# Two places in a hand-ordered schedule: the first shared-out unit behind a block, and the sink scores of the slots that end in a block

## The chip, the cores and the metric

The kernel runs on one core of one Trainium2 chip. The metric is the device time of one launch in microseconds, the median of 3 runs: 180.98 us (180.37, 180.98 and 181.20). The engines have short names in the profile: PE is TensorE (matrix products and transposes), PEld its weight loads, DVE is VectorE, ACT is ScalarE, POOL is GpSimd, and SP is the engine that starts most of the transfers. Each engine works through its own list of instructions in the order in which the kernel writes them, and waits on semaphores for the others.

## What is computed

Two layers, one after the other, for 4 sequences of 768 rows. The first is attention with 8 heads of 64 columns, in which a query sees the keys of the last 128 positions and the first 4 positions ("sinks"). The second is a gated block: a matrix product to 1024 columns, a gelu, one half normalised and mixed over the rows with a 768 x 768 matrix, a product of the halves, and a projection back, added to the input.

```
scores = scale * q @ k.T          # 4 x 8 heads, 768 x 768, 64 columns
keep   = (pos_k < 4) | (0 <= pos_q - pos_k < 128)
a      = softmax(where(keep, scores, -1e9));  x = a @ v       # -> 4 x 768 x 512
h      = gelu(x @ w_in);  u, v = halves of h
v_n    = (v - mean) / sqrt(var + 1e-6) * g_ln
v_s    = w_sg @ v_n + b_sg        # over the 768 rows
out    = x + (u * v_s) @ w_out
```

## The kernel before, in words

**Slots.** The main loop (L571) has 16 slots, one for each pair of heads; `n` is the slot, and four slots (HP = 4) make a sequence. A slot writes out, in this order, the work of several stages at once, because every engine keeps to the written order:

- For `g` = 0, 1, 2 (HT = 3): `score(n, g)` (L249) makes the scores of two key tiles on PE into a PSUM tile `sc`, and ACT takes their exponential into `ex` (L264). `keep_band(n, g)` (L266) multiplies that part of `ex` by a mask of ones and zeros on DVE (L271). This is "the mask" in what follows; the mask of `g` waits for the exponential of `g`.
- Between these stand the weighted sums of the pair before (`values`, L288: PE into `av`, then on DVE a reciprocal and the product `x`, L315 and L316), and the keys and queries of the next pair (`keys` L208, `queries` L216: six transposes on PE into `cps`, then a copy on ACT, L204). In a late slot (below) `queries` stands at `g` = 1.
- `sinks(n)` (L273) makes the scores of the sink keys with one 512-column product on PE (`scs`, L275), and ACT takes their exponential (`exs`, L277). It stands behind the three rounds.

The score tiles `sc` and `scs` share two PSUM buffers in turn, so the product that fills one waits for the exponential of the tile two places before.

**Blocks.** In slots 4, 8 and 12 (`n % HP == 0`, `n > 0`) the four pairs of a sequence are complete. There `columns(n - 1)` (L283: six transposes, a copy `xT` on DVE, L286) stands behind the last scores, and at the slot's end comes the block `hidden` (L422): 6 products `hv` (L333) with gelu (L335) and statistics (L337), with 3 of the weighted sums of slot `n` between them; 8 products `hu` (L345) with gelu (L348); and the normalisation `vn` (L373). A gelu needs another table on ACT than an exponential or a copy, and each change is an ACT_TABLE_LOAD.

**Units.** The rest of the second layer is put on a list of units, which later slots share out. Behind the first block these are 6 `spatial_weights` (L177: six transposes of `w_sg` on PE into `wps`, a copy `wsgT` on DVE, L182), behind every block 8 `spatial` (L377: six products `vs` on PE, then `gv`, L386, and `gT`, L389, on DVE) and 6 `project` (L391: four products `o_ps`, a sum `o_sb` on DVE, L401, and a store by SP). `wps`, `vs`, `o_ps`, `hv`, `hu` and, in some places, `cps` share two PSUM buffers of the pool `ps_m` in turn. `spread(left)` (L584) takes the next share off the list: two units at each of the four places of slot 5, one at each place of slot 9.

**Late slots.** The slot behind a block (5, 9 and 13; `late`) has only the second three weighted sums left. It writes, for `g` = 0: scores, keys, the three sums, mask 0, then the first share of units, `spread(HT + 1)`; for `g` = 1: scores, mask 1, the second share, queries; for `g` = 2: scores, mask 2, the third share; then the sinks, and the fourth share. PE has no part in a mask, and the units' products need no mask of their own slot; what a place of the mask decides is DVE's order.

Of the kernel before, what the change touches and what calls it, by code (L numbers as in the profile page):

```python
# [17 lines left out]
def kernel(  # L18
# [14 lines left out]
    nc = tc.nc  # L33

    B, H, S, Dh = q.shape
# [6 lines left out]
    HP = H // 2  # L42
# [18 lines left out]
    HT = NT // 2  # L61
    NS = S - 256
    NB = 2
# [3 lines left out]
    sk_bufs = [consts.tile([128, 128], BF16, name=f"sk{i}") for i in range(NB)]  # L67
# [17 lines left out]
    def load_v(n):  # L85
        b, hp = divmod(n, HP)
        nc.gpsimd.dma_start(  # L87
            out=v_bufs[n % NV][:, :, :, 0:64],
            in_=v[b, 2 * hp:2 * hp + 2].rearrange("h (t p) d -> p h t d", p=128))
# [69 lines left out]
    def load_weights(n):  # L159
        if n < 4:  # L160
            half = slice(DF, d_ff) if n < 2 else slice(0, DF)
            cs = slice(KD // 2 * (n % 2), KD // 2 * (n % 2 + 1))
            nc.gpsimd.dma_start(
                out=w_in_sb[:, cs, half],
                in_=moe_w_in.rearrange("(c p) f -> p c f", p=128)[:, cs, half])
        elif n == 4:
            for c in (slice(0, HT), slice(HT, NT)):
                nc.gpsimd.dma_start(
                    out=wsg_sb[:, c, :],
                    in_=moe_w_sg.rearrange("(c p) s -> p c s", p=128)[:, c, :])  # L170
        elif n == 5:
            nc.gpsimd.dma_start(out=b_bc, in_=moe_b_sg.partition_broadcast(128))
            nc.gpsimd.dma_start(out=g_sb, in_=moe_g_ln.rearrange("(c p) -> p c", p=128))
            nc.gpsimd.dma_start(out=w_out_sb,
                                in_=moe_w_out.rearrange("(c p) f -> p c f", p=128))
# [8 lines left out]
    packed, qTs, exps, avs = {}, {}, {}, {}  # L184
    x_sb, xT = {}, {}

    def repack(n, eng):
        packed[n] = []
        for src, name in zip(qk.pop(n), ("k_bf", "q_bf")):
            flat = work.tile([128, NT, 128], BF16, name=name)  # L190
            eng.tensor_copy(flat.rearrange("p t (h d) -> p h t d", h=2), src)  # L191
            packed[n].append(flat)
# [15 lines left out]
    def keys(n):  # L208
        kT, sk = kT_bufs[n % NB], sk_bufs[n % NB]
        kps = to_columns(packed[n][0], ps_t, "tp")  # L210
        copy(nc.scalar, kT, kps)
        for hl in range(2):
            rows = slice(64 * hl, 64 * hl + 64)
            nc.gpsimd.tensor_copy(sk[rows, 32 * hl:32 * hl + n_sink], kT[rows, 0:n_sink])  # L214

    def queries(n, eng, pool, tag):  # L216
        qps = to_columns(packed.pop(n)[1], pool, tag)
        qTs[n] = work.tile([128, S], BF16, name="qT")
        copy(eng, qTs[n], qps)
# [29 lines left out]
    def score(n, g):  # L249
        kT, qT = kT_bufs[n % NB], qTs[n]  # L250
        if g == 0:
            exps[n] = work.tile([128, NT * 512 - 256], BF16, name="ex")
        ex = exps[n]
        sc = ps_s.tile([128, 2, 512], F32, name="sc", tag="s")
        w = 0
        for j in (2 * g, 2 * g + 1):
            n_q = min(256, S - 128 * j)
            for hl in range(2):
                rows = slice(64 * hl, 64 * hl + 64)
                nc.tensor.matmul(sc[:, hl, w:w + n_q], kT[rows, 128 * j:128 * (j + 1)],  # L260
                                 qT[rows, 128 * j:128 * j + n_q], start=True, stop=True)
            w += n_q
        part = ex[:, 1024 * g:1024 * g + 2 * w].rearrange("p (h c) -> p h c", h=2)
        nc.scalar.activation(out=part, in_=sc[:, :, 0:w], func=AF.Exp, scale=scale)  # L264
# [7 lines left out]

    def sinks(n):  # L273
        scs = ps_s.tile([128, 2, 512], F32, name="scs", tag="s")
        nc.tensor.matmul(scs[:, 0, 0:NS], sk_bufs[n % NB], qTs.pop(n)[:, 256:S],  # L275
                         start=True, stop=True)
        nc.scalar.activation(out=exs_bufs[n % NB][0:32 + n_sink],  # L277
                             in_=scs[0:32 + n_sink, 0, 0:NS], func=AF.Exp, scale=scale)
# [4 lines left out]
    def columns(n, pool=ps_m, tag="mm"):  # L283
        b, hp = divmod(n, HP)
        xps = to_columns(x_sb[b][:, hp], pool, tag)
        nc.vector.tensor_copy(xT[b][:, hp, :], xps.rearrange("c t p -> c (t p)"))  # L286

    def values(n, i):  # L288
        b, hp = divmod(n, HP)
        if hp == 0 and i == 0:  # L290
            x_sb[b] = work.tile([128, HP, NT, 128], BF16, name="x")
            xT[b] = work.tile([128, HP, S], BF16, name="xT")
        ex, exs, v_sb = exps[n], exs_bufs[n % NB], v_bufs[n % NV]
        c, m = divmod(i, HT)
        if m == 0:
            avs[n] = ps_a.tile([128, HT, 2, 65], F32, name="av", tag="av")
        av = avs[n]

        def probs(j, hl, half):
            at = 1024 * (j // 2) + hl * min(512, S - 256 * (j // 2) + 128)  # L300
            at += 256 * (j % 2) + 128 * half
            return ex[:, at:at + 128]

        for hl in range(2):
            nc.tensor.matmul(av[:, m, hl, :], probs(i, hl, 0), v_sb[:, hl, i, :],  # L305
                             start=(m == 0 and hl == 0), stop=False)
            if i >= 1:
                nc.tensor.matmul(av[:, m, hl, :], probs(i - 1, hl, 1),  # L308
                                 v_sb[:, hl, i - 1, :], start=False, stop=False)
        if i >= 2:  # L310
            nc.tensor.matmul(av[:, m], exs[:, 128 * (i - 2):128 * (i - 1)],
                             vsink[:, n], start=False, stop=(m == HT - 1))
        if m == HT - 1:
            rcp = inverses[:, 2 * n + c]
            nc.vector.reciprocal(rcp, av[:, :, :, 64:65])  # L315
            nc.vector.tensor_mul(  # L316
                x_sb[b][:, hp, HT * c:HT * (c + 1), :].rearrange(
                    "p i (h d) -> p i h d", h=2),
                av[:, :, :, 0:64], rcp.to_broadcast([128, HT, 2, 64]))
        if i == NT - 1 and by_dma(n):  # L320
            nc.sync.dma_start_transpose(
                out=xT[b][:, hp, :].rearrange("p (i q) -> p i q", i=NT),
                in_=x_sb[b][:, hp].rearrange("p i d -> p (i d)"))
# [93 lines left out]
    def fill(count=1):  # L417
        for _ in range(count):
            if fillers:
                fillers.pop(0)()  # L420
# [150 lines left out]
    for n in range(NP):  # L571
        if n + 2 < NP:
            repack(n + 2, G)
            load_v(n + 2)
        load_weights(n)
        late = half_valued == n - 1

        def value(i):
            if n > 0 and (i >= HT or not late):
                values(n - 1, i)  # L580

        points = (HT + 1) * ((HP - n) % HP)

        def spread(left):  # L584
            if n > HP * (B - 1):
                fill(1 if left > 2 or (left == 1 and n < NP - 1) else 0)
            else:
                fill(-(-len(fillers) // (points + left)))

        for g in range(HT):  # L590
            if n + g > 0:
                score(n, g)
            if g < 2 and not late:
                for i in range(HT * g, HT * (g + 1)):
                    value(i)
            if g == 0 and n > 0 and n + 1 < NP:
                keys(n + 1)
                if n < HP:
                    queries(n + 1, A, ps_m, "mm")
            if g == 0 and late:  # L600
                for i in range(HT, NT):
                    value(i)
            if g == HT - 1 and n % HP == 0 and n > 0:
                columns(n - 1)
            keep_band(n, g)
            if g == 1 and late:
                spread(HT)
            if g == 1 and n + 1 < NP and n >= HP:
                queries(n + 1, A, ps_t, "tp")
            if g != 1 or not late:  # L610
                spread(HT + 1 - g)
        if n + 3 < NP:
            load_qk(n + 3)
        sinks(n)
        if n == 0:
            keys(1)
            queries(1, A, ps_m, "mm")
        if 0 < n < HP:
            columns(n - 1)
        spread(1)  # L620
        if n % HP == 0 and n > 0:
            fill(len(fillers))
            hidden(n // HP - 1, [lambda i=i: values(n, i) for i in range(HT)])
            half_valued = n
# [58 lines left out]
```

## Time and profile before

| | us |
|---|---|
| median of 3 runs (lowest, highest) | 180.98 (180.37, 181.20) |
| the profiled execution: its time | 180.05 |
| its span, first to last instruction | 178.3 |
| PE busy | 158.1 (89%) |
| DVE busy | 144.2 (81%) |
| ACT busy | 118.9 (67%) |
| POOL busy | 58.2 (33%) |

The span is what the views of the profile cover; 1.75 us of the profiled time lie outside it. All times below that name a place ("at 47.79") are us from the start of the span. In a line of the timeline the first two numbers are start and length, then come engine, line, operation, the tiles written and read, and the number of instructions; a bracket gives the idle time of the engine just before, and what ended it. Slot 5 begins at 43.6, slot 9 at 86.2, slot 13 at 123.5; the blocks before them begin at 31.3, 74.9 and 111.6 with their first `hv`.

### The profile page before, as it was taken

Reading aid. Unit: us, or ns where it says so; the run is one execution under the profiler, and the core shown is the slowest. Engines: PE = TensorE matmul, PEld = TensorE weight load, DVE = VectorE, ACT = ScalarE, POOL = GpSimd, SP = SyncE. Lnnn points to the kernel's source line nnn. Section 1 sums busy time; section 2 is a strip of 40 time slices with the busy share of each in tenths; the row PEclk is TensorE's granted clock in tenths of the full one; section 3 lists DMA queues with packets and bytes.
Section 4 is the critical chain, followed back from the end, with each engine's and each line's share of the span. In section 5 each row is a group of like instructions: output and inputs, shape, how many; then the busy total and the mean of one; then the engine's idle time right before and its main releaser. Section 6 shows DMA issues by size and latency. Waiting matters only on the chain.

```text
span 178.3 us, 3744 instructions
## 1 busy us (share of the span) xinstructions
PE 158.1 (89%) x1407; PEld 89.5 (50%) x1418; DVE 144.2 (81%) x359; ACT 118.9 (67%) x168; POOL 58.2 (33%) x98
## 2 busy tenths in 40 slices
PE   0769779899589999999999999899999999999970
PEld 0447556345456555445556546446465454546430
DVE  5664889599859999878899999599999949858950
ACT  2488999877746677677878678867996756640000
POOL 8549999950042060344007060353020000000000
PEclk9999999999969999999999999999999999999996
DMA  5999999999747539999073969997202241011071
GB/s 155 274 288 272 273 273 272 190 208 220 119 167 48 112 120 185 303 305 76 9 214 30 194 198 179 353 163 45 44 4 46 48 178 59 0 73 50 0 298 62
DMA packets 47974, 27.24 MB, mean 153 GB/s; under 512 B 33680, under 2 KB 44944, under 8 KB 47952
## 3 DMA queue, kind: packets, MB, share of 16 engines
q0 software_dynamic: 27904, 6.31, 37.7%
q1 hardware_dynamic: 19504, 20.26, 37.1%
q10 hardware_dynamic: 544, 0.39, 0.7%
q8 instruction: 12, 0.20, 0.4%
q14 instruction: 10, 0.08, 0.1%
HBM read 24.81 MB, written 6.29 MB: 174 GB/s over the span
## 4 chain that ended last, share of the span: by engine, by line
PE 53%; DVE 25%; ACT 12%; issue 4%; DMA 2%; DVEq 0%
PE hu L345 9%; PE o_ps L397 9%; PE vs L383 8%; PE hv L333 8%; ACT ex L264 6%; DVE gv L386 6%; PE sc L260 5%; DVE ex L271 5%; PE cps L197 4%; DVE gT L389 3%; PE av L305 3%; DVE x L316 3%; ACT qT L204 2%; DVE st L337 2%; DMA k_sb<-in_k_dram 2%
## 5 line engine op out<-in xcount | busy, mean ns | idle before, releaser
L264 ACT ACTIVATE ex<-sc 128x1024 bf16<-128x1024 f32 (+1 forms) x48 | 45.7, 960 | 16.8 <-PE sc L260 16.7
L383 PE MATMUL vs<-wsgT,vn 128*128 128x384 bf16 x192 | 35.8, 329 | 0.7 <-DVE wsgT L182 0.5
L191 POOL CAST k_bf<-k_sb 128x768 bf16<-128x768 f32 x15 | 12.8, 853 | 41.8 <-DMA k_sb<-in_k_dram 24.9
L397 PE MATMUL o_ps<-w_out_sb,gT 128*128 128x512 bf16 (+1 forms) x93 | 23.8, 370 | 0.8 <-DVE o_sb L401 0.4
L383 PEld LDWEIGHTS <-vn 128*128 128x128 bf16 x192 | 17.9, 99 | 13.0 <-issue 2.8
L271 DVE TENSOR_TENSOR ex<-ex,mask 128x1024 bf16<-128x1024 bf16 x32 | 22.6, 708 | 2.2 <-ACT ex L264 2.2
L345 PE MATMUL hu<-xT,w_in_sb 128*128 128x384 bf16 x128 | 23.2, 324 | 0.1
L333 PE MATMUL hv<-w_in_sb,xT 128*128 128x512 bf16 x92 | 22.0, 379 | 1.2 <-ACT v_all L335 0.9
L386 DVE SCALAR_TENSOR_TENSOR gv<-vs,g_sb,b_bc 128x384 bf16<-128x384 f32 x32 | 19.6, 612 | 2.1 <-PE vs L383 2.1
L260 PE MATMUL sc<-qT,kT 64*128 64x256 bf16 x192 | 19.0, 280 | 2.3 <-DVE qT L240 1.3
L337 DVE BATCH_NORM_STATS2 st<-v_all 128x6 f32<-128x512 f32 x24 | 16.2, 676 | 5.6 <-ACT v_all L335 5.6
L348 ACT ACTIVATE uT<-hu 128x384 bf16<-128x384 f32 x32 | 15.7, 491 | 6.5 <-PE hu L345 6.3
L316 DVE TENSOR_TENSOR x<-av,inverses 128x384 bf16<-128x384 f32 x32 | 17.8, 558 | 1.1
L305 PE MATMUL av<-v_sb,ex 128*128 128x65 bf16 x192 | 18.2, 198 | 0.5 <-DVE x L316 0.2
L305 PEld LDWEIGHTS <-ex 128*128 128x128 bf16 x192 | 14.4, 100 | 7.9 <-issue 2.9
L335 ACT ACTIVATE v_all<-hv 128x512 f32<-128x512 f32 x24 | 14.1, 597 | 6.0 <-PE hv L333 6.0
L345 PEld LDWEIGHTS <-w_in_sb 128*128 128x128 bf16 x128 | 12.4, 96 | 10.7 <-issue 2.9
L87 POOL DMA_DIRECT2D v_sb<-in_v_dram x16 | 16.6, 1038 | 0.0
L308 PE MATMUL av<-v_sb,ex 128*128 128x65 bf16 x160 | 16.5, 197 | 0.0
L214 POOL COPY sk<-kT 64x4 bf16<-64x4 bf16 x30 | 6.6, 221 | 29.3 <-ACT kT L204 28.4
L333 PEld LDWEIGHTS <-xT 128*128 128x128 bf16 x96 | 9.1, 98 | 11.3 <-issue 1.4
L191 POOL CAST q_bf<-q_sb 128x768 bf16<-128x768 f32 x15 | 13.9, 930 | 1.7 <-DMA q_sb<-in_q_dram 1.1
(83 smaller groups left out, 241.9 us busy)
## 6 DMA issues: line engine op xcount, KB each, us to landing
k_sb<-in_k_dram SPq DMA_DIRECT2D x15, 384.0 KB, 5.5
q_sb<-in_q_dram SPq DMA_DIRECT2D x15, 384.0 KB, 6.0
out_dram<-o_sb SPq DMA_DIRECT2D x17, 256.0 KB, 3.8
v_sb<-in_v_dram POOLq DMA_DIRECT2D x16, 192.0 KB, 6.6
out_dram<-o_act SPq DMA_DIRECT2D x6, 256.0 KB, 2.0
wsg_sb<-in_moe_w_sg_dram POOLq DMA_DIRECT2D x2, 576.0 KB, 9.8
w_in_sb<-in_moe_w_in_dram POOLq DMA_DIRECT2D x4, 256.0 KB, 8.8
w_out_sb<-in_moe_w_out_dram POOLq DMA_DIRECT2D x1, 512.0 KB, 10.8
```

Of the source, the lines that this page charges most:

```text
L191: eng.tensor_copy(flat.rearrange("p t (h d) -> p h t d", h=2), src)
L260: nc.tensor.matmul(sc[:, hl, w:w + n_q], kT[rows, 128 * j:128 * (j + 1)], qT[rows, 128 * j:128 * j + n_q], start=True, stop=True)
L264: nc.scalar.activation(out=part, in_=sc[:, :, 0:w], func=AF.Exp, scale=scale)
L271: nc.vector.tensor_mul(part, part, m)
L305: nc.tensor.matmul(av[:, m, hl, :], probs(i, hl, 0), v_sb[:, hl, i, :], start=(m == 0 and hl == 0), stop=False)
L316: nc.vector.tensor_mul(x_sb[b][:, hp, HT * c:HT * (c + 1), :].rearrange("p i (h d) -> p i h d", h=2), av[:, :, :, 0:64], rcp.to_broadcast( ...
L333: nc.tensor.matmul(h_ps, xT[b][:, c, 128 * j:128 * (j + 1)], w_in_sb[:, c, DF:], start=(c == 0), stop=(c == KD - 1))
L337: nc.vector.bn_stats(out=st, in_=v_alls[b][:, j, :])
L345: nc.tensor.matmul(h_ps[:, 0:NH], w_in_sb[:, c, 128 * f:128 * (f + 1)], xT[b][:, c, NH * n:NH * (n + 1)], start=(c == 0), stop=(c == KD - 1))
L383: nc.tensor.matmul(vs[:, 0:NH], vns[b][:, si, 128 * f:128 * (f + 1)], wsgT[:, si, cols], start=(si == 0), stop=(si == NT - 1))
L386: nc.vector.scalar_tensor_tensor(out=gv, in0=vs[:, 0:NH], scalar=g_sb[:, f:f + 1], in1=b_bc[:, cols], op0=ALU.mult, op1=ALU.add)
L397: nc.tensor.matmul(o_ps, gTs[b][:, c, rows], w_out_sb[:, c, cols], start=(c == 0), stop=(c == KU - 1 and whole))
```

## The change

In late slots the first share of units is written ahead of mask 0 instead of behind it. In slots 4, 8 and 12 the sinks are written ahead of the third scores instead of behind the third round; in these slots the product `scs` thereby takes the PSUM buffer that the third `sc` had, and the other way round. All other slots keep their order. The number of instructions is the same, and so is the number of units in each share. `sinks` no longer takes `qT` off its table, since the scores behind it still read it; that is bookkeeping of the program that writes the kernel, and no instruction.

```diff
     def sinks(n):
         scs = ps_s.tile([128, 2, 512], F32, name="scs", tag="s")
-        nc.tensor.matmul(scs[:, 0, 0:NS], sk_bufs[n % NB], qTs.pop(n)[:, 256:S],
+        nc.tensor.matmul(scs[:, 0, 0:NS], sk_bufs[n % NB], qTs[n][:, 256:S],
                          start=True, stop=True)
...
         for g in range(HT):
+            if g == HT - 1 and n % HP == 0 and n > 0:
+                sinks(n)
             if n + g > 0:
                 score(n, g)
...
             if g == 0 and late:
                 for i in range(HT, NT):
                     value(i)
+                spread(HT + 1)
             if g == HT - 1 and n % HP == 0 and n > 0:
                 columns(n - 1)
             keep_band(n, g)
...
-            if g != 1 or not late:
+            if g == 2 or not late:
                 spread(HT + 1 - g)
         if n + 3 < NP:
             load_qk(n + 3)
-        sinks(n)
+        if n % HP > 0 or n == 0:
+            sinks(n)
```

## The prediction

> **What bounds the kernel now.** I read the page's busy shares, then the chain of waits, then the timeline around the three blocks, then a table of granted clock by stages. The chain is, by engine:
>
> ```profile
> PE 53%; DVE 25%; ACT 12%; issue 4%; DMA 2%; DVEq 0%
> ```
>
> PE is the floor nearly everywhere; DVE carries the chain from 113 to 141 us. So an edit pays where PE stands still, or where DVE does between 113 and 141. The longest halt that the chain crosses is in slot 5, behind the first block, and the change touches it. The timeline there, with some rows left out:
>
> ```profile
> 45.39 0.56 DVE L316 TENSOR_TENSOR x<-av,inverses 128x384 bf16<-128x384 f32 x1
> ...
> 46.57 0.69 DVE L271 TENSOR_TENSOR ex<-ex,mask 128x1024 bf16<-128x1024 bf16 x1 [0.62 <-ACT ex L264]
> ...
> 47.12 1.04 ACT L264 ACTIVATE ex<-sc 128x1024 bf16<-128x1024 f32 x1
> 47.18 1.02 DVE L182 COPY wsgT<-wps 128x768 bf16<-128x768 bf16 x2
> ...
> 47.79 0.96 PE L180 MATMUL wps<-iden,wsg_sb 128*128 128x128 bf16 x12 [1.81 <-DVE wsgT L182]
> ...
> 48.19 0.69 DVE L271 TENSOR_TENSOR ex<-ex,mask 128x1024 bf16<-128x1024 bf16 x1
> ...
> 48.80 1.01 DVE L182 COPY wsgT<-wps 128x768 bf16<-128x768 bf16 x2
> 49.12 0.80 ACT L204 COPY qT<-cps 128x768 bf16<-128x768 bf16 x1 [0.96 <-PE cps L197]
> 49.81 0.82 ACT L264 ACTIVATE ex<-sc 128x768 bf16<-128x768 f32 x1
> 50.66 0.56 DVE L271 TENSOR_TENSOR ex<-ex,mask_end 128x768 bf16<-128x768 bf16 x1 [0.85 <-ACT ex L264]
> 51.14 1.01 DVE L182 COPY wsgT<-wps 128x768 bf16<-128x768 bf16 x2
> ```
>
> DVE has `x` done at 45.95 and then idles 0.62 us for the exponential behind the table load, although the copies of two finished `wps` stand next. PE, whose third `wps` needs the buffer that the first copy empties, idles 1.81 us. The queries' transposes stand behind that `wps`, so ACT idles 0.96 us ahead of `qT`; so exponential 2 is late, so mask 2 is late (0.85), so the copies behind it, and the first `vs` waits for the fifth of them (51.69) and starts at 51.74.
>
> **Part one, slot 5.** No instruction comes or goes; two copies of 0.55 us (0.47 from start to start) pass mask 0 (0.69). Step by step:
>
> 1. Copies 1 and 2 start at 45.87 and 46.34, 0.48 behind the start of `x`, a spacing that slot 8 has (71.12, 71.60). They end at 46.42 and 46.89. Mask 0 follows at 46.8; its input is there since 46.54, and it is read only in slot 6.
> 2. PE's third and fourth `wps` start at 46.49 and 46.96 instead of 47.79 and 48.25; the transposes of the queries follow at 47.3 instead of 48.58 (their buffer is free when the copy `kT` ends at 47.23).
> 3. ACT is in exponential 1 until 48.16, as before. Then `qT` at 48.05 instead of 49.12, exponential 2 from 48.73 to 49.55 instead of 49.81 to 50.63.
> 4. Mask 1 does not move: it waits for exponential 1 (48.19). Copies 3 and 4 stay at 48.80 and 49.27.
> 5. Mask 2 follows copy 4 directly, at 49.74 instead of 50.66; copies 5 and 6 at 50.22 and 50.69; the first `vs` at 50.83 instead of 51.74. Gain **0.91 us**. Late next is DVE, which is full from mask 1 on.
>
> Behind that, PE was busy 14.73 of the 15 us from 60 to 75, so the gain should be carried on. The transfers do not take it back: `k_sb` for slot 8 is cast at 51.18 and its transposes come in slot 7; the cast at 104.13 is done 1.9 us before its transposes at 107.22, twice the gain. Nothing on SP is passed: the transposing transfer waits for `x`, which stays.
>
> **The clock in this place** is the uncertain term. Windows on the grid of the granted clock:
>
> ```profile
> 25.32:28.73 3.41, 2.36 (x39) 1.61 (x37) 2.85 (x8) 3.37 (x5) 3.29 (x6) 1.00 1.60 254
> ...
> 45.80:49.21 3.41, 1.60 (x26) 1.24 (x22) 2.79 (x6) 2.45 (x4) 0.37 (x2) 1.00 0.65 96
> 49.21:52.62 3.41, 2.90 (x20) 1.89 (x17) 2.10 (x5) 2.01 (x3) 1.31 (x2) 0.50 0.59 213
> ```
>
> The columns are window, length, then busy us of PE, PEld, DVE, ACT, POOL, then the granted clock. A stretch with PE busy 1.60 of 3.41 us was followed by 3.41 us at half clock; one with 2.36 was not. With the steps above the same stretch has some 1.77 (estimate), between the two rows but nearer to the first. If the half-clock stretch stays at its place, transposes go at 0.107 us instead of 0.055 and `scs` at 0.43, so PE itself reaches `vs` only at 51.12; the stretch then covers 1.5 us of `vs` instead of 0.9, and the twelve products end at 53.88 instead of 54.20: gain 0.32. If it goes, the twelve take 2.00 us (0.162 apart) instead of 2.46: gain 0.91 + 0.46 = 1.37. I take 0.91, which leaves the clock's toll as it was, and keep 0.32 and 1.37 as ends.
>
> The Trainium skill, "TensorE: Matmul & The Clock Gate" (Part 1 and Part 4), says that the activity window of about 3.4 us runs freely and that transposes do not count as busy in the same way. By it the stretch would stay slow, since transposes are all that the change draws into it. The 3.41 agrees; whether transposes count no row decides alone (the 1.60 holds 0.37 of other products, the 2.36 holds 1.77).
>
> **Part one, slots 9 and 13.** Slot 9:
>
> ```profile
> 89.16 0.69 DVE L271 TENSOR_TENSOR ex<-ex,mask 128x1024 bf16<-128x1024 bf16 x1 [0.77 <-ACT ex L264]
> ...
> 89.70 1.04 ACT L264 ACTIVATE ex<-sc 128x1024 bf16<-128x1024 f32 x1
> ...
> 90.77 0.69 DVE L271 TENSOR_TENSOR ex<-ex,mask 128x1024 bf16<-128x1024 bf16 x1
> ```
>
> `gv` and `gT` can use the 0.77 us: `vs` is done at 88.54. But mask 1 waits for exponential 1, which ends at 90.74; it stays at 90.77, and so does all behind it. PE is in no need of the buffer before 90.56. **Zero.** In slot 13 `x` ends at 126.47, exponential 0 at 126.44 and `vs` at 126.17: everything is ready, DVE is full, and the order of a sum does not change it. **Zero**, give or take 0.05.
>
> **Part two, slots 4, 8, 12.** On ACT `exs` (0.47 from start to start) and exponential 2 (0.82) change places. Slots 4 and 12: ACT is full from `qT` (slot 4) or from the third scores (slot 12) to the table load, and the load comes after both: zero in slot 4; 0.05 lost in slot 12, as `scs` takes 0.38 to its end and `sc` 0.34. New wait: the third `sc` now needs the buffer of exponential 1, which ends at 30.59 (slot 4, 0.33 after `sc` started), 71.27 (0.72 before) and 109.97 (0.71 before). Behind it on PE stand `columns` and `hv`; in slot 4 they have cover, since `hv` is done at 32.5 and gelu waits for the table until 33.74. Slot 8:
>
> ```profile
> 73.28 0.55 DVE L271 TENSOR_TENSOR ex<-ex,mask_end 128x768 bf16<-128x768 bf16 x1
> 74.00 0.69 DVE L401 TENSOR_TENSOR o_sb<-o_ps,x 128x512 f32<-128x512 f32 x1 [0.17 <-PE o_ps L397]
> ...
> 74.21 0.59 ACT L277 ACTIVATE exs<-scs 36x512 bf16<-36x512 f32 x1 [1.03 <-PE scs L275]
> ```
>
> ACT's 1.03 us of idling goes, and the table is loaded at 75.1 instead of 76.10; but the first `hv` ends only at 75.9, so gelu wins 0.2, and PE does not wait for it: `hv` 3 followed the weighted sums directly (76.98). Against it, exponential 2 now ends near 73.75, mask 2 starts 0.5 later at 73.78, `o_sb` at 74.26 instead of 74.00 ends at 74.95, and the first `hv`, which takes its buffer, starts at 75.0 instead of 74.87. **0.1 lost** (bounds: 0.2 won, 0.3 lost).
>
> **Sum.** -0.91 + 0 + 0 + 0 + 0.1 + 0.05 = -0.76 us. The profiled execution would go from 180.05 to 179.29; the median shown is 0.93 above the profiled run, and I put the difference on it: 180.98 - 0.76 = **180.2 us**.
>
> **Rivals.**
>
> - *The clock keeps its slow stretch* and the queue's gain is half eaten: 0.32 - 0.15 = 0.17 won, 180.8 us. For: PE's work drawn into the stretch is only 0.17 us. Against: its idle time is cut from one piece of 1.81 into 0.5 and 1.1, and the grid lies anywhere.
> - *The slow stretch goes*: 1.37 - 0.15 = 1.22 won, 179.8 us.
> - *Slower: sinks delay the block.* If the third `sc`, held by its new buffer wait, comes later than `exs` ends, ACT no longer swaps two neighbours but inserts 0.59 ahead of the table load. Three slots make 1.77; less 0.91 that is 0.86 lost, 181.8 us. It decides where the table loads of slots 4 and 12 come over 0.3 us later, counted from `qT`. Against it stand the 0.7 us of slack in slots 8 and 12, and in slot 4 that `qT` keeps ACT until 31.27, behind the 30.59.
> - *It does nothing*: DVE's list in slot 5 is held by another semaphore (the copies wait for something I do not see), gain 0, 181.1 us.
>
> **Numbers.** Forecast 0.42, slow stretch kept 0.25, gone 0.18, slower 0.10, nothing 0.05. A measurement of this kernel can tell about 0.5%, 0.9 us, from no change; that bound lies at 180.08, just below the forecast, whose own spread of some 0.3 us puts 0.17 of its chance beyond. Faster: 0.18 + 0.17 = 0.35; slower 0.10; within 0.55. Range 179.5 to 181.2: it takes in the kept stretch and no effect, most of the gone one, and leaves out the slower case and the lowest tail.
>
> **What would show it.** Right: in slot 5 two `wsgT` copies directly behind `x` and ahead of mask 0; PE's 1.81 us of idling cut to about 0.5; no idle ACT ahead of `qT`; the first `vs` 4.9 us behind the end of `x` instead of 5.8 (5.2 if the slow stretch stays). In slot 9 DVE's mask 1 still right behind exponential 1. In slots 4 and 12 the table load as far behind `qT` as before; in slot 8 about 1 us nearer, with no earlier `hv`. Wrong: a clock row of another kind in slot 5; `hv` later by 0.3 or more in any block; or PE halts between 55 and 75 that eat the gain.

## The result, and the profile after

The changed kernel takes 178.75 us, the median of 20 runs; before, run beside it 20 times, takes 180.29. The ratio is 0.9937 (95% interval 0.9915 to 0.9959): 0.63% faster, 1.14 us, with 0.7 to 1.5 inside the interval. All ratios, and all counts and group medians by the clock below, leave out executions that took over 1.5% longer than the fastest of their kernel. The two medians lie further apart than the ratio says, 1.54 us; why is answered below, with the clock. The forecast was 0.76 us and 180.2 us, with 179.5 as the low end. The direction was right, the size by the ratio half again as large as forecast, and the time lies 0.75 us below the range. Of the miss of 1.45 us in the time, 0.69 is the base: the median of 3 runs from which I counted, 180.98, was 180.29 over 20.

The profiled execution of the changed kernel took 178.66 us, span 176.9 (before 180.05 and 178.3). The chain by engine:

```profile
PE 58%; DVE 20%; ACT 10%; issue 5%; POOL 3%; DMA 2%; POOLq 0%; DVEq 0%; ACTq 0%
```

PE carries more of it, DVE less. The timeline of slot 5 after the change, with the rows that answer to those shown of before:

```profile
45.14 0.56 DVE L316 TENSOR_TENSOR x<-av,inverses 128x384 bf16<-128x384 f32 x1
...
45.62 1.01 DVE L182 COPY wsgT<-wps 128x768 bf16<-128x768 bf16 x2
...
46.22 0.96 PE L180 MATMUL wps<-iden,wsg_sb 128*128 128x128 bf16 x12 [0.48 <-DVE wsgT L182]
46.55 0.68 DVE L271 TENSOR_TENSOR ex<-ex,mask 128x1024 bf16<-128x1024 bf16 x1
46.88 1.04 ACT L264 ACTIVATE ex<-sc 128x1024 bf16<-128x1024 f32 x1
...
47.79 0.82 ACT L204 COPY qT<-cps 128x768 bf16<-128x768 bf16 x1
...
47.95 0.69 DVE L271 TENSOR_TENSOR ex<-ex,mask 128x1024 bf16<-128x1024 bf16 x1 [0.72 <-ACT ex L264]
48.47 0.86 ACT L264 ACTIVATE ex<-sc 128x768 bf16<-128x768 f32 x1
48.56 1.01 DVE L182 COPY wsgT<-wps 128x768 bf16<-128x768 bf16 x2
49.16 0.96 PE L180 MATMUL wps<-iden,wsg_sb 128*128 128x128 bf16 x12 [1.35 <-DVE wsgT L182]
49.49 0.55 DVE L271 TENSOR_TENSOR ex<-ex,mask_end 128x768 bf16<-128x768 bf16 x1
49.96 1.01 DVE L182 COPY wsgT<-wps 128x768 bf16<-128x768 bf16 x2
...
50.56 2.11 PE L383 MATMUL vs<-wsgT,vn 128*128 128x384 bf16 x12 [0.22 <-DVE wsgT L182]
```

Before, the row of these first twelve `vs` was:

```profile
51.74 2.53 PE L383 MATMUL vs<-wsgT,vn 128*128 128x384 bf16 x12 [0.47 <-DVE wsgT L182]
```

The copies stand ahead of mask 0, PE's halt at the third `wps` fell from 1.81 to 0.48 us, ACT no longer idles ahead of `qT`, and mask 2 follows copy 4. A new halt of 1.35 us stands at the fifth `wps`: copy 3 is behind mask 1, and mask 1 waits 0.72 us for exponential 1. The first `vs` starts at 50.56, 5.42 us behind the start of `x` (before: 51.74 and 45.39, 6.35 us), and the twelve take 2.11 us instead of 2.53.

Where the two executions part is seen when the same instruction is looked up in both. The offset "after less before" on ACT's instructions is -0.24 us up to the end of block 1, but for the two that were swapped in slot 4 (it is there from 19 us on, ahead of all that the change touches, and so is no gain of the change), then -0.93 at slot 5's `exs`, -1.60 at slot 6's first exponential, -1.60 until slot 8, -1.24 from the second `hv` of block 2 on, and -1.20 at the last `gelu`. So slot 5 wins 1.36, slot 8 gives back 0.36, and the rest is level but for 0.2 either way.

### The profile page after: what moved, and what is told of

It reads as the page before. It is cut to its first block, busy times and chain, and to the rows that moved or that the text cites. A ratio compares the mean times of both kernels' runs of the same rounds, so it can differ in the third digit from the quotient of the medians.

```text
span 176.9 us, 3760 instructions
## 1 busy us (share of the span) xinstructions
PE 157.6 (89%) x1418; PEld 88.6 (50%) x1418; DVE 144.9 (82%) x359; ACT 118.7 (67%) x168; POOL 58.5 (33%) x98
## 4 chain that ended last, share of the span: by engine, by line
PE 58%; DVE 20%; ACT 10%; issue 5%; POOL 3%; DMA 2%; POOLq 0%; DVEq 0%; ACTq 0%
PE vs L383 12%; PE o_ps L397 10%; PE hu L345 10%; PE hv L333 9%; ACT ex L264 5%; PE sc L260 5%; DVE ex L271 4%; PE cps L197 4%; PE av L305 3%; DVE gv L386 3%; DVE x L316 2%; DVE st L337 2%; DMA k_sb<-in_k_dram 2%; ACT kT L204 2%; DVE gT L389 2%
## 5 line engine op out<-in xcount | busy, mean ns | idle before, releaser
L191 POOL CAST k_bf<-k_sb 128x768 bf16<-128x768 f32 x15 | 13.7, 910 | 40.9 <-DMA k_sb<-in_k_dram 37.5
L214 POOL COPY sk<-kT 64x4 bf16<-64x4 bf16 x30 | 7.1, 237 | 27.6 <-ACT kT L204 26.7
L408 ACT COPY o_act<-o_ps 128x512 f32<-128x512 f32 (+1 forms) x7 | 3.7, 549 | 15.7 <-PE o_ps L405 15.7
```

## The experiments

Each kernel was timed against before on one chip. Each execution has a mean granted clock. One stretch of 3.41 us at half clock takes 1.71 of 178 us, 0.0096, off that mean, so executions fall into two groups: 0.990 and above (no such stretch in the middle of the kernel), and 0.981 to 0.989 (with one). The border is not sharp: one profile below (all three shares with the sinks) has 0.989 and no such stretch, so an execution at 0.989 can be sorted wrongly.

**The change once more, and before, by the clock.**

> The changed kernel once more, beside the next three. My theory: 0.6 to 0.8 us below before where both have no slow stretch in slot 5 (mean granted clock 0.99 or more), no gain where both have it (0.989 or less), and the slow stretch in fewer of its executions than of before's; together 0.4% to 0.8% faster.

Ratio 0.9926 (0.9897 to 0.9955). By groups (number, median us):

| | without the stretch | with it |
|---|---|---|
| before, beside this run | 11, 179.40 | 15, 180.20 |
| before, beside the next four | 14, 179.31 | 18, 180.07 |
| before, beside the last four | 2, 180.12 | 8, 180.17 |
| the change, first 20 runs | 16, 178.69 | 3, 180.15 |
| the change, this run | 10, 178.58 | 2, 179.50 |

Without the stretch the change wins 0.82 us beside this run; the stretch costs before 0.80 and 0.76 (the two runs without it beside the last four are too few); and before has it in 41 of 68 executions, the change in 5 of 31. The share alone is worth about (0.60 - 0.16) x 0.8 = 0.35 us on the mean (an estimate). With the stretch in both, five runs of the change are too few to say what is won.

Why the shares differ can be read from the two profiles. The most work of PE in a window of 3.41 us that half clock followed in slot 5 of any profile here is 1.73 us. In before a window holds no more than that if it starts anywhere from 44.24 to 46.14, in the change only from 45.60 to 45.89. If the grid of these windows lies anywhere with the same chance, that is 56% and 9% of the executions (an estimate), beside the 60% and 16% that the clock shows.

This profile shows the case: the stretch is there, and `vs` starts 5.67 us behind the start of `x` and 5.1 behind its end; I gave 5.2 for that case. Slot 5 wins 0.25 us in it (offset -0.17 before, -0.42 behind).

**Part one alone.**

```diff
             if g == 0 and late:
                 for i in range(HT, NT):
                     value(i)
+                spread(HT + 1)
...
-            if g != 1 or not late:
+            if g == 2 or not late:
                 spread(HT + 1 - g)
```

> Part one alone: the first share of units ahead of mask 0 in slots 5, 9 and 13, the sinks where they were. My theory now (order of DVE's copies in slot 5 wins 0.9 us, a rarer slow clock stretch there adds to it, the sinks lose some 0.3 us in slot 8): faster than before by 1.2 to 1.6 us, some 0.3 us more than the whole change's 1.14. Rival (order only, the clock's toll is the same in both kernels): faster by 0.9. Rival (the gain is that of the sinks): 0.

Ratio 0.9961 (0.9924 to 0.9997); 178.54 us without the stretch (7 runs), 179.94 with it (4). By the ratio that is 0.7 us, not the 1.2 to 1.6 that I expected. Without the stretch part one wins 0.77, as much as the whole change; that it wins 0.3 more than the change is not borne out. The stretch came in 4 of 11 executions, more than the change had, though the windows that would bring it are as few in its profile (starts from 45.67 to 45.95); that stays open. Its profiled execution has the stretch, and there slot 5 wins 0.30 us (offset -0.17 before, -0.47 behind), where the prediction has 0.32 for this case.

```profile
45.67:49.08 3.41, 1.73 (x26) 1.37 (x23) 2.67 (x6) 3.41 (x5) 0.39 (x2) 1.00 0.87 128
49.08:52.49 3.41, 3.26 (x18) 2.12 (x18) 2.10 (x5) 0.90 (x2) 0.97 (x2) 0.50 0.70 231
```

These are windows on the clock's grid, as in the prediction: PE busy 1.73 us, then half clock (0.50) just where `vs` now runs. In the profiled execution of the change the grid lies otherwise:

```profile
44.53:47.94 3.41, 2.80 (x44) 2.18 (x42) 2.66 (x7) 3.40 (x5) 0.40 (x2) 1.00 0.97 160
47.94:51.35 3.41, 1.96 (x18) 1.29 (x18) 3.02 (x6) 1.98 (x3) 0.26 (x1) 1.00 0.85 244
```

Neither of these windows has less than 1.96, and the clock stays. So the two kernels' profiles differ by the place of the grid as well as by the change.

**Part two alone.**

```diff
+            if g == HT - 1 and n % HP == 0 and n > 0:
+                sinks(n)
             if n + g > 0:
                 score(n, g)
...
-        sinks(n)
+        if n % HP > 0 or n == 0:
+            sinks(n)
```

> Part two alone: the sinks ahead of the third scores in slots 4, 8 and 12, units where they were. My theory: slower by 0.1 to 0.4 us, all of it in slot 8, where mask 2 and the sum o_sb come later and the first hv with them; slots 4 and 12 within 0.05. Rival (the earlier table load is worth something): faster by 0.2 or more.

Ratio 1.0026 (0.9993 to 1.0059): no gain, and a loss of 0.1 to 0.4 is inside the interval but not shown. In its profile slots 8 and 12 are level (offsets 0.26 to 0.27, and 0.27 to 0.27). Slot 4 lost 0.32, in a wait of PE for the transfer of `v_sb` (1.0 us); the same wait, 1.2 us, stands in the profile of a kernel below that leaves the sinks alone (two shares ahead), so it need not be theirs.

**Only the clock: work in PE's idle time.** To before, work was added on PE in slot 5 behind the second scores, into the PSUM tile that is then free; its result is never read.

```diff
+    def warm(count):
+        w = ps_a.tile([128, HT, 2, 65], F32, name="warm", tag="av")
+        for _ in range(count):
+            nc.tensor.matmul(w.rearrange("p a b c -> p (a b c)")[:, 0:384], iden,
+                             w_in_sb[:, 0, 0:384], start=True, stop=True)
...
             keep_band(n, g)
+            if g == 1 and n == HP + 1:
+                warm(6)
```

> Before, with six products of 384 columns added on PE in the 1.81 us in which it idles in slot 5; their result is never read. Nothing else waits for them. If the slow clock stretch of slot 5 comes from PE's idling and costs what the before trace shows: mean granted clock up by about 0.01, the twelve vs 0.162 us apart, and a time 0.4 to 1.0 us below before, though no copy and no vs input is earlier. If the clock has no part in the gain: 0, or up to 0.3 us slower.

The other kernel has `nc.tensor.transpose` of blocks of `w_sg` in place of the products, 18 of them.

> Before, with 18 transposes added on PE in the same idle time (about as long as the six products of the other run); their result is never read. If transposes count as activity for the clock as products do: the same gain as with the six products, 0.4 to 1.0 us. If they do not count: clock and time as before, within 0.2 us.

With products: ratio 1.0018 (0.9976 to 1.0059); with transposes: 0.9979 (0.9955 to 1.0003). The clock did what was expected: not one of 23 executions has the stretch, against 18 of 32 of before beside them; a 24th, with products and at 183.46 us, has 0.988. The windows of the one with transposes:

```profile
45.32:48.73 3.41, 2.78 (x43) 2.19 (x44) 2.77 (x6) 2.53 (x3) 0.37 (x2) 1.00 0.99 109
48.73:52.15 3.42, 2.21 (x23) 1.44 (x23) 2.27 (x5) 2.09 (x3) 0.86 (x2) 1.00 0.82 249
```

Transposes hold the clock as well as products do. In both profiles slot 5 wins 0.42 us with no copy earlier, near the 0.46 that I had put on the stretch. The times do not show the 0.4 to 1.0 that I expected: the transposes win 0.36 us by the medians, not clear of noise, and the products nothing. Beside the executions of before without the stretch (179.31), the two kernels are 0.16 and 0.48 us slower, so the added work is not free. Three runs with products came at 181.4 to 181.7 with a full clock, and what slowed them is open.

**How far the order carries.** In late slots the first two shares, and then all three, were written ahead of their masks; sinks as in before.

```diff
+            if g < 2 and late:          # all three: if late
+                spread(HT + 1 - g)
             keep_band(n, g)
-            if g == 1 and late:
-                spread(HT)
...
-            if g != 1 or not late:
+            if g == 2 or not late:      # all three: if not late
                 spread(HT + 1 - g)
```

> Part one carried on to the second share: in late slots the first and second shares ahead of masks 0 and 1, sinks as in before. If the chain that I read in slot 5 is right (copies 5 and 6 stand behind mask 2, mask 2 behind exponential 2, and that is fixed by ACT), the first vs of slot 5 comes only 0.1 to 0.2 us earlier than with the first share alone, though two more copies are 1.3 us earlier; slot 9 wins 0.2 to 0.3 as mask 1 no longer holds the second gv. Time 0.3 to 0.5 us below that of part one alone. Rival (every copy taken past a mask is worth its wait): 1 us or more below part one alone.

> Part one carried on to all three shares ahead of the three masks of late slots, sinks as in before. My theory: copies 5 and 6 of slot 5 no longer wait for exponential 2, the first vs starts 2.0 to 2.3 us earlier than in before, PE has no 3.41 us with under 1.9 us of work there, so the mean granted clock is 0.99 or more in nearly all executions; time 2.0 to 3.0 us below before. Rival (the masks, now behind everything, hold the sums of the next slots): 1 us or less below before.

Two shares: ratio 0.9953 (0.9919 to 0.9987), 178.63 us without the stretch, 0.77 below before without it, as part one alone; the 0.3 to 0.5 more that I expected are not there. `vs` of slot 5 starts 5.43 us behind `x`, against 5.42 with one share. The reason is the row that I had read for it:

```profile
49.78 0.56 DVE L271 TENSOR_TENSOR ex<-ex,mask_end 128x768 bf16<-128x768 bf16 x1 [0.71 <-ACT ex L264]
50.25 1.02 DVE L182 COPY wsgT<-wps 128x768 bf16<-128x768 bf16 x2
```

Mask 2 waits for exponential 2, and copies 5 and 6 stand behind it, however early copies 3 and 4 were. Slot 9 won its 0.28 in the profile (offset -1.30 to -1.58), but half of it was gone at slot 10.

All three: ratio **0.9832 (0.9790 to 0.9874)**, 176.66 us, all six executions without the stretch. The same kernel once more, beside the last experiments:

> All three shares ahead of the masks in late slots, sinks as in before, once more: 2.8 to 3.4 us below before (1.5% to 1.9%), mean granted clock 0.99 or more in nearly all executions.

Ratio 0.9785 (0.9724 to 0.9847), 176.86 us; before 180.27. Five of the six executions are without the stretch; the sixth, at 180.31 us, has 0.982. Slot 5 of the first of the two:

```profile
48.13 0.69 DVE L271 TENSOR_TENSOR ex<-ex,mask 128x1024 bf16<-128x1024 bf16 x1
...
48.74 1.02 DVE L182 COPY wsgT<-wps 128x768 bf16<-128x768 bf16 x2
49.34 0.97 PE L383 MATMUL vs<-wsgT,vn 128*128 128x384 bf16 x5 [0.36 <-DVE wsgT L182]
...
49.67 0.55 DVE L271 TENSOR_TENSOR ex<-ex,mask_end 128x768 bf16<-128x768 bf16 x1
```

`vs` starts 4.15 us behind `x`, 2.20 earlier than before; PE halts 0.35 us at the third `wps` and 0.36 at `vs`, where before it halted 1.81 and 0.47; mask 2 comes last and ends at 50.22, 3.6 us before the next weighted sums. Neither window of the grid there has PE busy under 3.0 us. This version beats both kernels.

**Slot 5 alone**, all three shares ahead of the masks there and nowhere else (`late` in the first condition replaced by `n == HP + 1`):

> Shares ahead of the masks in slot 5 alone; slots 9 and 13 and the sinks as in before. If all of the gain is the copies of w_sg in slot 5: as fast as the run with all late slots, within 0.2 us. Rival (DVE's idling behind each block counts): 0.3 us or more slower than that run.

Ratio 0.9824 (0.9770 to 0.9879). By the medians it is 0.6 us above the kernel with all late slots, more than the 0.2 expected, but the intervals cover each other. In the four profiles with all late slots, slot 9 wins 0.27 or 0.28 us in three (in one of them half of it is gone a slot later) and loses 0.08 in the fourth, and slot 13 moves by 0.03 or less; what the two slots are worth in the time stays open.

**What part two costs, without the stretch.** Part two was added to the kernel with all three shares ahead; then mask 2 of slots 4, 8 and 12 was written behind the slot's last share, so that it stands ahead of no `o_sb`. The second was also done on part two alone.

```diff
+            ends = g == HT - 1 and n % HP == 0 and n > 0
+            if not ends:
+                keep_band(n, g)
-            keep_band(n, g)
...
         spread(1)
         if n % HP == 0 and n > 0:
+            keep_band(n, HT - 1)
             fill(len(fillers))
```

> The same with part two of the change (sinks ahead of the third scores in slots 4, 8 and 12), to weigh part two where no slow clock stretch blurs it. If part two costs what I put into the sum for slots 8 and 12: 0.1 to 0.2 us above the run without it. If it helps: below it. If the 0.36 us that the changed kernel's profile lost in slot 8 is the rule and not a chance meeting of mask 2 with a cast on POOL: 0.3 to 0.4 above.

> The same as the run before with sinks, but in slots 4, 8 and 12 mask 2 is written behind the slot's last share of units. If mask 2 on DVE is the only cost of part two: as fast as the run without part two, within 0.15 us; PE then wins nothing from the sinks.

> Part two alone, but in slots 4, 8 and 12 mask 2 is written behind the slot's last share of units, so that it holds no o_sb on DVE. If mask 2 behind the later exponential is what part two costs in slot 8: first hv of slot 8 no later than in before, time within 0.2 us of before, some 0.3 below part two alone. If part two costs something else or nothing: no difference to part two alone.

Ratios: 0.9800 (0.9738 to 0.9863) with the sinks, 0.9812 (0.9756 to 0.9869) with mask 2 late as well, 0.9785 without part two. No difference is resolved, and no help of part two is shown. On part two alone, mask 2 late gave 0.9996 (0.9967 to 1.0024). The offsets in slot 8, the last thing before it to the second `hv`, are clearer than the times: with the sinks first, 0.36 lost in the first profile of the change, and 0.01 or less in the three others; with mask 2 late 0.15 **won** in both, though in one of them mask 2 took 1.10 us beside a cast. The 0.36 is shown by these rows of the changed kernel:

```profile
71.76 0.82 POOL L191 CAST k_bf<-k_sb 128x768 bf16<-128x768 f32 x1 [6.52 <-DMA k_sb<-in_k_dram]
...
72.09 0.91 DVE L271 TENSOR_TENSOR ex<-ex,mask_end 128x768 bf16<-128x768 bf16 x1
72.92 1.28 DVE L401 TENSOR_TENSOR o_sb<-o_ps,x 128x512 f32<-128x512 f32 x2
...
73.65 1.02 PE L333 MATMUL hv<-w_in_sb,xT 128*128 128x512 bf16 x4 [0.43 <-DVE o_sb L401]
```

Mask 2 takes 0.91 us instead of 0.55 beside a cast on POOL; `o_sb` is late by that, and PE halts 0.43 us for the buffer of the first `hv`. In the second profile of the change the cast came at nearly the same time, 71.78, and slot 8 itself 1.2 us later; mask 2 took 0.56, and `hv` did not wait:

```profile
73.26 0.56 DVE L271 TENSOR_TENSOR ex<-ex,mask_end 128x768 bf16<-128x768 bf16 x1
73.74 1.39 DVE L401 TENSOR_TENSOR o_sb<-o_ps,x 128x512 f32<-128x512 f32 x2
...
74.48 1.02 PE L333 MATMUL hv<-w_in_sb,xT 128*128 128x512 bf16 x4
```

## Why the prediction was right and wrong

- **Slot 5's chain, steps 1 to 5: right.** `vs` was forecast 5.44 us behind the start of `x` (50.83 less 45.39) and came at 5.42; each of the steps stands in the timeline. That the copies behind mask 2 are the limit was borne out twice: two shares ahead made `vs` no earlier, three made it 1.3 us earlier than that.
- **The clock: this step failed.** "I take 0.91, which leaves the clock's toll as it was" treated the stretch as one thing that stays or goes, though the prediction itself says that the grid lies anywhere. It is a lottery: the grid lies at another place in each execution, and in before more places are unlucky (41 of 68 executions) than in the change (5 of 31). The sum had nothing for this share. On the mean it is some 0.35 us, and 0.76 + 0.35 is the 1.11 beside a measured 1.14. On the median, which is the metric, it is some 0.7 (estimates, since the first 20 runs of before have no clock on record): the median of before lies among its executions with the stretch (180.2) and that of the change among those without (178.7), so the medians part by 1.5. Among executions without the stretch the sum held: 0.82 won, for 0.76. The two ends that I worked out were both met by profiles: 1.36 in slot 5 where the stretch went (forecast 1.37), 0.30 and 0.25 where it stayed (0.32).
- **The base: wrong by 0.69 us.** Three runs that lie 0.8 us apart are no base for a range of 1.7 us, and the range left no room for that; what made these three longer is not shown, since their clocks are not on record. From 180.29 the same sum gives 179.53, still 0.78 above the time; that rest is near the 0.7 estimated for the clock.
- **Slots 9 and 13: right.** Mask 1 of slot 9 still starts right behind exponential 1, and the offset stays at -1.24 through slot 9. Slot 13 differs by 0.18, but that is lost in the block ahead of it, in two small operations beside POOL's work (0.47 and 0.68 us where before took 0.17 each, less one that took 0.78 in before and 0.17 here), and not in the second profile of the change.
- **Part two: right in slots 4 and 12, mis-sized in slot 8.** The table loads of slots 4 and 12 moved by nothing, so the 0.05 put on slot 12 was nothing too. In slot 8 the mechanism was the one described, mask 2 ahead of `o_sb` and `hv`; its size was 0.36 in the one profile where mask 2 met a cast and 0.01 or less in the others, for my 0.1 with 0.3 as the end. The table load of slot 8 came 1.15 us earlier, as forecast, and won nothing. Rivals "sinks delay the block" and "it does nothing": not seen.
- **The rule of the skill.** The Trainium skill, "TensorE: Matmul & The Clock Gate" (Part 4), has transposes not count as activity in the same way as products. Here they do: 18 transposes alone removed the stretch in 12 of 12 executions.

## What to carry to other kernels

When a halt behind a stage is found, ask of every instruction in the waiting engine's list who needs it soon: here the masks were needed a slot later and the copies at once. Freeing the first two copies won 0.8 us, the next two nothing, and only the last two, which `vs` waited for, brought it another 1.3 us forward. Count base and change by the same number of runs, and look at the granted clock of each: if executions fall into two groups, the share of each group is a term of the sum. Where an edit only swaps two neighbours on an engine, as the sinks do, ask what is late behind the pair: here the earlier table load of slot 8 was worth nothing, since nothing behind it was waiting for it alone.

## What the runs showed of the hardware

- **The activity that holds the clock.** A window of 3.41 us with PE busy 1.60, 1.62 or 1.73 us was followed by half clock; one with 1.78, 1.93, 1.96 or 2.21 was not. Where the kernel leaves no window of slot 5 with less than 1.78 (two shares ahead), 2.2 (added work) or 2.7 (all three shares), at whatever place the grid lies, the stretch came in 0 of 9, 0 of 23 and 0 of 11 executions. The windows of slot 5 started at places from 44.5 to 46.7 in the profiles. That transposes count is shown by a window with 0.34 us of other work in 1.93 that kept the clock, beside one with 0.37 in 1.60 that lost it.
- **Masks beside casts.** A mask (two inputs from SBUF) takes 0.55 or 0.68 us, never over 0.70 away from POOL's casts in any profile here, and up to 1.35 beside one; `gT`, also with two inputs from SBUF, 0.36 and up to 1.01. `x`, `gv`, `o_sb` and `wsgT`, which read PSUM, keep their times beside a cast. The Trainium skill, "SBUF — State Buffer" (Who interferes with whom), says that such an operation and GpSimd take turns at a shared pair of ports for whole instructions; the rows agree, and masks that met a cast without loss are among them.
- **Copies and tables.** A copy on ACT needs no other table than a gelu, although the description of the kernel says that it does: behind the table load at 140.98 in before, ACT runs a gelu at 142.28, four copies `o_act` from 142.39 to 146.46 and the gelus of the last block from 146.69 on without a further load. It is between exponential and gelu that each change shows a load of 1.28 us.
